# The sign of a float64 weight: a mask on VectorE, or a copy to float16 on ScalarE

## The chip, the cores and the metric

One core of one Trainium2 chip runs the whole program. The time is device microseconds of one execution, the median over several; the kernel before has three runs, 1212.31, 1214.31 and 1215.85 us. The profile is of one more execution.

## The reference

Three stages run one after the other, each on the output of the one before:

```python
# attention: q, k, v of 4 x 8 heads x 768 x 64, 4 sinks, window 128, float32
keep = is_sink | in_window
scores = np.where(keep, scale * (q @ k.T), -1e9)
a = softmax(scores);  x = a @ v            # -> 3072 tokens x 512

# MLP: w_in (512 x 2048) and w_out (2048 x 512) are float64
h = x @ w_in
g = h - np.tanh(h)
y = g @ w_out                              # -> float32

# MoE: 8 experts, 384 tokens each, assigned greedily by the sorted logits
logits = y @ w_gate
out[tok] = np.maximum(y[tok] @ w1[e], 0) @ w2[e]
```

`w_in` and `w_out` are a float32 array times a NumPy scalar, which makes them float64, and the kernel is given them so.

## The kernel before

TensorE multiplies in a reduced float32 format, so every float32 operand is split into a leading part and a remainder, and a product is three matmuls (leading by leading, remainder by leading, leading by remainder).

The tokens are worked on in eight units of 384. For each unit `u` a loop over 16 blocks `f` of the hidden size does `mlp_h` (lines 368 to 388: `h`, the tanh on ScalarE, `g`, `gh`, `gl`) and `mlp_y` (lines 390 to 414, line 402 is its matmul). Between these steps the attention of the next unit is spread: `scores` (line 269; matmuls 278 and 279, VectorE's line 287, ScalarE's exponential 288, VectorE's reciprocal 292, scaling 298), `transp` (319 to 322, tiles `ath` and `atl`), `sinks` (324; ScalarE makes the first half of `skT` in line 331, VectorE the second in 332) and `av` (335; matmul 351, then `xt` on ScalarE in 359, `xf` on VectorE in 360, `xh` in 363 on ScalarE, `xl` in 364 on VectorE). The matmul with `skT` is the last of each sum of `av`.

The float64 weights lie in DRAM as pairs of 32-bit words, and each piece is loaded as such a pair tile: 128 partitions x 1024 weights x 2 words. `leading` makes float32 of a piece. Word 1 holds the sign, the exponent and the upper bits of the mantissa. ScalarE scales it by 2^-112 as if it were a float32 (line 127), which leaves the exponent where an integer shift by three needs it. VectorE shifts word 0 right by 29, so that three bits are left (line 128), then puts the sign, which the later shift of word 1 would lose, into bit 31 of word 0 by a mask (line 129), and joins the two words by shift and or (line 131). The halves of a pair are counted 0 to 3 by the name `half`; half 3 is the upper half of word 1, half 1 the upper half of word 0, so bit 15 of half 1 is bit 31 of word 0.

`leading` is called 24 times: eight times in `split_win` for `w_in` (tile `winr`), eight in `split_wout` for `w_out` (tile `wor`), both before 180 us, and eight times in `gate_weights` (tile `wtr`), which works out `w_out` times `w_gate` between 300 and 560 us while the units 2 to 4 run. After each call ScalarE copies the leading part out (lines 146, 165, 454) and GpSimd subtracts for the remainder (147, 166, 455). The pair tiles of `w_out` and of the gates share one buffer, and the result of `leading` has two.

The order of the instructions on each engine is set by the framework's scheduler for the attention, the MLP and the gates; each engine then runs its list strictly in that order. The MoE part behind it is written out in an order of its own.

Of the kernel before, what the change touches and what calls it, by code (L numbers as in the profile page):

```python
# [10 lines left out]
F32 = mybir.dt.float32  # L11
F32R = mybir.dt.float32r
I32 = mybir.dt.int32
U16 = mybir.dt.uint16
BF = mybir.dt.bfloat16
F16 = mybir.dt.float16
AF = mybir.ActivationFunctionType
OP = mybir.AluOpType
# [15 lines left out]
def raw(t):  # L34
    return t.bitcast(F32)
# [3 lines left out]
def attn_mlp_moe(ctx, tc, qT, kP, v, w_in, w_out, w_outT, w_gate, w1, w2, out):  # L39
    nc = tc.nc  # L40
# [81 lines left out]
    def leading(pairs, n):  # L122


        hi, lo = pairs[:, :, :, 1], pairs[:, :, :, 0]
        half = pairs.rearrange("p a b t -> p a (b t)").bitcast(U16).rearrange("p a (b t) -> p a b t", t=4)
        nc.scalar.activation(raw(hi), raw(hi), AF.Copy, scale=2.0 ** -112)
        nc.vector.tensor_scalar(lo, lo, 29, None, op0=OP.logical_shift_right)
        nc.vector.tensor_scalar(half[:, :, :, 1], half[:, :, :, 3], 0x8000, None, op0=OP.bitwise_and)
        t = st.tile([P] + n, I32, name="f1")  # L130
        nc.vector.scalar_tensor_tensor(t, hi, 3, lo, op0=OP.logical_shift_left, op1=OP.bitwise_or)
        return t.bitcast(F32)
# [10 lines left out]
    def split_win(j):  # L143
        f1 = leading(WINR[j], [NC, 256])
        t = wts.tile([P, 2, NC, 256], F32R, name=f"win{j}", tag=f"win{j}")
        nc.scalar.copy(t[:, 0], f1)
        nc.gpsimd.tensor_sub(t[:, 1], f1, raw(t)[:, 0])
        WIN[j] = t
# [13 lines left out]
    def split_wout(j):  # L162
        f1 = leading(WOR[j], [2, C])
        t = wop.tile([P, 2, C], F32R, name=f"wo{j}")
        nc.scalar.copy(t, f1)
        nc.gpsimd.tensor_sub(f1, f1, raw(t))
        nc.sync.dma_start(wol_d[2 * j:2 * j + 2].rearrange("f p c -> p f c"), f1)
        WO[2 * j], WO[2 * j + 1] = t[:, 0], t[:, 1]
# [278 lines left out]
    def gate_weights(j):  # L447
        t = st.tile([P, NC, 256, 2], I32, name="wtr", tag="wor", bufs=1)
        nc.sync.dma_start(t.rearrange("p c f t -> p c (f t)"),
                          w_outT.bitcast(I32).rearrange("(c p) f -> p c f", p=P)[:, :, j * 512:(j + 1) * 512])  # L450
        yield
        f1 = leading(t, [NC, 256])
        t = st.tile([P, 2, NC, 256], F32R, name="wts_", tag="wor", bufs=1)
        nc.scalar.copy(t[:, 0], f1)
        nc.gpsimd.tensor_sub(t[:, 1], f1, raw(t)[:, 0])
        yield
        o = psA.tile([P, 512], F32, name="o")[:16, :256]
        for c in range(NC):
            for h in range(2):
                nc.tensor.matmul(o, wg[:, c], t[:, h, c], start=(c + h == 0), stop=(c == NC - 1 and h == 1))  # L460
        r = st.tile([16, 256], F32, name="wpr", tag="f1")
        nc.scalar.copy(r, o)
        yield
        t = psA.tile([P, 2, 16], F32, name="wpt", tag="t")
        for h in range(2):
            nc.tensor.transpose(t[:, h], r[:, h * P:(h + 1) * P], ident[:16, :16])
        s1 = st.tile([P, 2, 8], F32, name="wps", bufs=1)
        s2 = st.tile([P, 2, 8], F32, name="wpq", bufs=1)
        nc.scalar.copy(s1, t[:, :, 8:])
        nc.vector.tensor_add(s2, t[:, :, :8], s1)  # L470
        d = WPS[:, 2 * j:2 * j + 2]
        nc.vector.tensor_copy(d[:, :, :8], s2)
        nc.vector.tensor_sub(d[:, :, 8:], s2, raw(d)[:, :, :8])
        yield
# [43 lines left out]
    pairs = [(u, p) for u in range(NU) for p in range(4)]  # L518
# [650 lines left out]
```

## Time and profile before

| what | value |
|---|---|
| median of three runs | 1214.31 us |
| profiled execution: time, span | 1212.97 us, 1211.3 us |
| mean granted TensorE clock | 0.964 |
| busy share: TensorE, VectorE, ScalarE, GpSimd | 92%, 65%, 52%, 42% |
| line 129: runs, busy in total | 24, 38.88 us |

The span runs from the first to the last instruction; what the profiled execution took beyond it lies around it. The busy shares are over the whole span. The granted clock is the share of TensorE's full speed that the chip allowed, 1.00 in most of the run and less in the first 180 us.

### The profile page before, as it was taken

The numbers are of one execution on the slowest core, as the hardware profiler recorded it, in microseconds if no ns is written. First come the engines' busy times: TensorE is split into PE (matmuls) and PEld (weight loads), VectorE is DVE, ScalarE is ACT, GpSimd is POOL, SyncE is SP. The second block draws the span as 40 slices with busy tenths as digits, with TensorE's granted clock in tenths as the row PEclk, the third lists the DMA queues.
The fourth block names the chain that finished last, engine by engine and source line by source line (L and its number), as shares of the span: only waits on it lengthen the run. The fifth ranks groups of instructions, "written<-read, shape, count | busy, mean of one in ns | idle before, by whom it ended". The sixth has DMA issues, their size and how long they took to land.

```text
span 1211.3 us, 19574 instructions
## 1 busy us (share of the span) xinstructions
PE 1119.3 (92%) x6484; PEld 950.3 (78%) x6484; DVE 788.1 (65%) x2164; ACT 634.5 (52%) x1541; POOL 513.7 (42%) x616
## 2 busy tenths in 40 slices
PE   4677799999999999999999999998989999998997
PEld 3456588888888778888888888886677888887986
DVE  6779985656756667565665665455787878778321
ACT  6876666556655566665655665441224433343421
POOL 6367653324333344334332333100137765676830
PEclk9868989999999999999999999998979999998999
DMA  7554454233442434342332322111634564346500
GB/s 215 174 167 163 163 191 119 78 83 114 129 132 68 132 96 131 117 144 73 102 91 76 116 77 81 44 44 30 223 116 129 166 192 140 100 145 209 171 30 27
DMA packets 87606, 145.29 MB, mean 120 GB/s; under 512 B 9680, under 2 KB 32208, under 8 KB 87504
## 3 DMA queue, kind: packets, MB, share of 16 engines
q1 hardware_dynamic: 83664, 131.45, 35.5%
q0 software_dynamic: 3840, 12.59, 3.2%
q8 instruction: 51, 0.84, 0.3%
q14 instruction: 51, 0.42, 0.1%
HBM read 127.22 MB, written 16.78 MB: 119 GB/s over the span
## 4 chain that ended last, share of the span: by engine, by line
PE 71%; DVE 5%; issue 3%; DMA 3%; ACT 2%; POOL 1%; POOLq 0%; SPq 0%; ACTq 0%; DVEq 0%
PE y L402 18%; PE h L976 10%; PE o L1003 6%; PE h L375 6%; PE h L373 6%; PE h L374 6%; PE o L351 4%; PE o L1007 3%; PE t L319 2%; DMA wtr<-in_w_outT_dram 2%; PE s L278 2%; PE s L279 1%; DMA wl<-wol_d 1%; PE search L678 1%; PE o L429 1%
## 5 line engine op out<-in xcount | busy, mean ns | idle before, releaser
L891 POOL TENSOR_TENSOR w<-wraw,w 128x512 fp32r<-128x512 f32 x120 | 150.9, 1287 | 84.6 <-ACT w L885 83.6
L373 PE MATMUL h<-xh,win 128*128 128x384 f32 x512 | 178.7, 350 | 0.4 <-ACT xh L363 0.3
L375 PE MATMUL h<-xh,win 128*128 128x384 f32 x512 | 178.1, 348 | 0.0
L374 PE MATMUL h<-xl,win 128*128 128x384 f32 x512 | 175.4, 343 | 1.7 <-DVE xl L364 1.7
L976 PE MATMUL h<-mxh,w 128*128 128x384 f32 x512 | 147.1, 346 | 0.0
L402 PE MATMUL y<-wo,gl 128*128 128x512 f32 x336 | 141.5, 422 | 0.0
L402 PE MATMUL y<-wl,gh 128*128 128x512 f32 x336 | 136.3, 406 | 0.0
L402 PE MATMUL y<-wo,gh 128*128 128x512 f32 x336 | 134.9, 403 | 1.5 <-ACT gh L386 1.5
L300 POOL TENSOR_SCALAR a<-a,stat 128x260 f32<-128x260 f32 (+2 forms) x168 | 94.6, 576 | 79.7 <-DVE stat L292 74.0
L288 ACT ACTIVATE a<-sm,stat 128x260 f32<-128x260 f32 (+2 forms) x192 | 94.5, 492 | 40.9 <-DVE stat L287 38.3
L287 DVE CUSTOM_DVE_ANT_0 sm<-s,m 128x260 f32<-128x260 f32 (+2 forms) x192 | 76.9, 401 | 51.6 <-PE s L279 43.1
L1003 PE MATMUL o<-w,hh 128*128 128x512 f32 x384 | 108.7, 404 | 0.0
L982 ACT ACTIVATE hh<-h 128x384 fp32r<-128x384 f32 x64 | 31.5, 492 | 142.3 <-PE h L976 137.4
L373 PEld LDWEIGHTS h<-xh,win 128*128 128x128 f32 x512 | 97.7, 191 | 7.2 <-ACT xh L363 1.5
L374 PEld LDWEIGHTS h<-xl,win 128*128 128x128 f32 x512 | 97.8, 191 | 6.9 <-DVE xl L364 2.5
L380 DVE TENSOR_TENSOR g<-h,g 128x384 f32<-128x384 f32 x128 | 71.2, 556 | 46.9 <-ACT g L379 46.3
L250 POOL TENSOR_TENSOR kl<-k,kh 128x388 fp32r<-128x388 f32 (+1 forms) x64 | 81.3, 1277 | 45.8 <-ACT kh L249 45.8
L375 PEld LDWEIGHTS h<-xh,win 128*128 128x128 f32 x512 | 97.9, 191 | 2.5 <-issue 1.5
L379 ACT ACTIVATE g<-h 128x384 f32<-128x384 f32 x128 | 62.1, 485 | 68.9 <-PE h L375 64.0
L976 PEld LDWEIGHTS h<-mxh,w 128*128 128x128 f32 x512 | 94.1, 191 | 2.4
L264 POOL TENSOR_TENSOR vs<-vr,vs 128x192 fp32r<-128x192 f32 (+1 forms) x64 | 46.5, 733 | 114.2 <-ACT vs L263 113.3
L885 ACT CAST w<-wraw 128x512 fp32r<-128x512 f32 x128 | 73.5, 619 | 38.4 <-DMA wraw<-in_w_dram 38.1
(261 smaller groups left out, 2646.1 us busy)
## 6 DMA issues: line engine op xcount, KB each, us to landing
wl<-wol_d SPq DMA_DIRECT2D x128, 256.0 KB, 2.8
wraw<-in_w_dram SPq DMA_DIRECT2D x128, 256.0 KB, 3.6
k<-in_k_dram SPq DMA_DIRECT2D x64, 131.0 KB, 2.9
winr<-in_w_in_dram SPq DMA_DIRECT2D x8, 1024.0 KB
wor<-in_w_out_dram SPq DMA_DIRECT2D x8, 1024.0 KB, 4.9
wtr<-in_w_outT_dram SPq DMA_DIRECT2D x8, 1024.0 KB, 5.7
k<-in_k_dram SPq DMA_DIRECT2D x64, 97.0 KB, 2.5
q<-in_q_dram SPq DMA_DIRECT2D x32, 192.0 KB, 2.7
```

The lines of the kernel that those rows point to most:

```text
L250: nc.gpsimd.tensor_sub(kl[:, :kn], k2[:, :kn], raw(kh)[:, :kn])
L287: nc.vector.tensor_tensor_reduce(sm[:, :n], s[:, :n], m, 1.0, 3e38, OP.add, OP.min, r[:, 0, hh:hh + 1])
L288: nc.scalar.activation(a[:, hh, :n], sm[:, :n], AF.Exp, bias=r[:, 0, hh:hh + 1], scale=-1.0, accum_out=r[:, 1, hh:hh + 1])
L300: nc.gpsimd.tensor_scalar(a[:, j, :n], a[:, j, :n], r[:, 3, j:j + 1], 1.0, op0=OP.mult, op1=OP.mult)
L373: nc.tensor.matmul(hp, w, xh[:, c], start=(c == 0), stop=False)
L374: nc.tensor.matmul(hp, w, xl[:, c], start=False, stop=False)
L375: nc.tensor.matmul(hp, win(f, 1, c), xh[:, c], start=False, stop=(c == NC - 1))
L402: mm = nc.tensor.matmul(y, m[:, ts], w, start=(f == 0 and w is hi and m is gh), stop=(f == NF - 1 and m is gl))
L885: nc.scalar.copy(W[n, q][:, 0, a], WR[n, q, a])
L891: (dve if mine else nc.gpsimd).tensor_sub(t[:, 1], r, raw(t)[:, 0])
L976: nc.tensor.matmul(hp, w[:, h, c, fs], x[:, c], start=(c + k == 0), stop=(c == NC - 1 and k == 2))
L1003: nc.tensor.matmul(o, hh[:, t * P:(t + 1) * P], w, start=(f + k == 0), stop=False)
```

## The change

The mask on VectorE goes. In its place ScalarE copies the scaled word 1, read as float32, into half 1 read as float16. The scaled word's magnitude is about 2^-112, far under the least float16, so that the copy yields a zero with the word's sign: bit 15 set or not.

```diff
--- before.py
+++ after.py
@@ -11,7 +11,6 @@
 F32 = mybir.dt.float32
 F32R = mybir.dt.float32r
 I32 = mybir.dt.int32
-U16 = mybir.dt.uint16
 BF = mybir.dt.bfloat16
 F16 = mybir.dt.float16
 AF = mybir.ActivationFunctionType
@@ -123,10 +122,11 @@
 
 
         hi, lo = pairs[:, :, :, 1], pairs[:, :, :, 0]
-        half = pairs.rearrange("p a b t -> p a (b t)").bitcast(U16).rearrange("p a (b t) -> p a b t", t=4)
+        half = pairs.rearrange("p a b t -> p a (b t)").bitcast(F16).rearrange("p a (b t) -> p a b t", t=4)
         nc.scalar.activation(raw(hi), raw(hi), AF.Copy, scale=2.0 ** -112)
         nc.vector.tensor_scalar(lo, lo, 29, None, op0=OP.logical_shift_right)
-        nc.vector.tensor_scalar(half[:, :, :, 1], half[:, :, :, 3], 0x8000, None, op0=OP.bitwise_and)
+
+        nc.scalar.copy(half[:, :, :, 1], raw(hi))
         t = st.tile([P] + n, I32, name="f1")
         nc.vector.scalar_tensor_tensor(t, hi, 3, lo, op0=OP.logical_shift_left, op1=OP.bitwise_or)
         return t.bitcast(F32)
```

The copy of line 129 reads what line 127's scaling wrote (both on ScalarE), and writes into the word that VectorE's shift has written, so it waits for the shift; VectorE's line 131 then waits for the copy. In the new kernel the scaling is line 126, the shift line 127; the other lines keep their numbers.

VectorE in the second gate, the shift of `wtr` to line 360's first addition, as a piece of the difference from before to after:

```order
 L322 TENSOR_TENSOR atl<-t,ath 128x2x256
-L128 TENSOR_SCALAR wtr<-wtr 128x1024
-L380 TENSOR_TENSOR g<-h,g 128x384
-L129 TENSOR_SCALAR wtr<-wtr 128x1024
+L127 TENSOR_SCALAR wtr<-wtr 128x1024
+L380 TENSOR_TENSOR g<-h,g 128x384
 L332 TENSOR_TENSOR skT<-s,skT 8x384
 L387 TENSOR_TENSOR gl<-g,gh 128x384
 L131 SCALAR_TENSOR_TENSOR f_3882<-wtr 128x1024
-L360 TENSOR_TENSOR xf<-o,xt 64x384 x2
```

The mask that stood ahead of `skT` (line 332) has gone, and the join of line 131 stays behind `gl` (line 387).

ScalarE in the same place, from the tanh of line 379 to `xt` of line 359:

```order
 L379 ACTIVATE g<-h 128x384
-L127 ACTIVATE wtr<-wtr 128x1024
-L331 CAST skT<-s 8x384
-L386 CAST gh<-g 128x384
+L126 ACTIVATE wtr<-wtr 128x1024
+L331 CAST skT<-s 8x384
+L386 CAST gh<-g 128x384
+L129 CAST wtr<-wtr 128x1024
 L359 COPY xt<-o 64x384
```

The new copy (CAST) stands behind `skT` and `gh`, and ahead of `xt`.

ScalarE in the early part, among the splits of `w_in` and `w_out` (`winr_392` is a pair tile, `f_806` a joined float32 piece):

```order
-L359 COPY xt<-o 64x384
-L127 ACTIVATE winr_392<-winr_392 128x1024
-L359 COPY xt<-o 64x384
-L288 ACTIVATE a,stat<-sm,stat 128x260
-L321 CAST ath<-t 128x2x256
+L359 COPY xt<-o 64x384 x2
+L129 CAST wor<-wor 128x1024
+L363 CAST xh<-xf 128x384
+L129 CAST winr_392<-winr_392 128x1024
 L165 CAST wo_808<-f_806 128x1024
-L363 CAST xh<-xf 128x384
```

Before, a scaling of `winr` and the weight copy of line 165 stood between the first `xt` (359) and `xh` (363); now it is the new copy for `wor` that stands between them.

## Rows read from the trace of the kernel before

**Rows 1.** The page's first part: busy us, share of the span, instructions.

```profile
PE 1119.3 (92%) x6484; PEld 950.3 (78%) x6484; DVE 788.1 (65%) x2164; ACT 634.5 (52%) x1541; POOL 513.7 (42%) x616
```

**Rows 2.** Windows: length, busy us (count) by engine, granted clock, DMA share, GB/s.

```profile
30.00:60.00 30.00, 18.49 (x79) 14.71 (x78) 23.41 (x64) 24.08 (x77) 9.60 (x11) 0.83 0.53 169
60.00:90.00 30.00, 21.63 (x81) 16.45 (x81) 23.17 (x41) 22.07 (x52) 18.30 (x15) 0.66 0.55 175
90.00:150.00 60.00, 46.16 (x219) 37.13 (x217) 57.12 (x69) 37.44 (x73) 43.60 (x32) 0.91 0.49 165
150.00:180.00 30.00, 27.13 (x135) 23.76 (x136) 24.56 (x46) 20.11 (x47) 16.67 (x16) 0.89 0.53 180
180.00:300.00 120.00, 119.80 (x666) 103.81 (x666) 72.98 (x190) 74.46 (x204) 40.66 (x68) 1.00 0.35 100
300.00:560.00 260.00, 249.88 (x1404) 213.73 (x1403) 169.64 (x413) 162.07 (x414) 99.49 (x137) 0.99 0.38 115
```

**Rows 3.** Windows of line 129's instructions alone: length, VectorE busy us (count).

```profile
0.00:60.00 60.00, 5.97 (x3) 0.91 0.62 192
60.00:90.00 30.00, 4.46 (x3) 0.66 0.55 175
90.00:150.00 60.00, 15.22 (x8) 0.91 0.49 165
...
300.00:560.00 260.00, 10.58 (x8) 0.99 0.38 115
```

**Rows 4.** Line 129 by tile: ns least, median, most; first and last start us.

```profile
L129 DVE TENSOR_SCALAR winr<-winr x8: 1309/1454/3332, 12.0 to 116.1; 128x1024 uint16<-128x1024 uint16 x8
...
L129 DVE TENSOR_SCALAR wtr<-wtr x8: 1305/1324/1336, 314.0 to 544.6; 128x1024 uint16<-128x1024 uint16 x8
```

**Rows 5.** Timeline, 96 us: start, us, engine, line, operation.

```profile
96.12 2.41 POOL L166 TENSOR_TENSOR f<-f,wo 128x1024 f32<-128x1024 f32 x1
...
96.38 3.33 DVE L129 TENSOR_SCALAR winr<-winr 128x1024 uint16<-128x1024 uint16 x1
```

**Rows 6.** Line 127, tile wor: ns least, median, most.

```profile
L127 ACT ACTIVATE wor<-wor x8: 1140/1156/1171, 71.3 to 170.9; 128x1024 f32<-128x1024 f32 x8
```

**Rows 7.** Line 146: ns least, median, most.

```profile
L146 ACT CAST win<-f x8: 1030/1042/1048, 26.1 to 141.3; 128x1024 fp32r<-128x1024 f32 x8
```

**Rows 8.** TensorE's waits, 60 to 180 us: us in total, times, longest.

```profile
PE s L278 <- DVE stat L287: 7.9, 5, 3.6
...
PE o L351 <- DVE atl L322: 3.0, 1, 3.0
```

**Rows 9.** Timeline, 30 to 34 us; in brackets the idle time before and its releaser.

```profile
30.38 3.10 DVE L129 TENSOR_SCALAR winr<-winr 128x1024 uint16<-128x1024 uint16 x1
...
33.99 0.77 PE L319 MATMUL t<-ident,a 128*128 128x128 f32 x2 [3.08 <-ACT a L298]
```

**Rows 10.** TensorE's waits, 300 to 560 us.

```profile
PE o L351 <- DVE skT L332: 7.4, 7, 1.8
PE o L351 <- DVE xf L360: 1.5, 3, 0.8
```

**Rows 11.** Timeline of gate 2 (its load landed at 337.08).

```profile
338.14 0.45 ACT L331 CAST skT<-s 8x384 fp32r<-8x384 f32 x1
...
338.31 1.31 DVE L129 TENSOR_SCALAR wtr<-wtr 128x1024 uint16<-128x1024 uint16 x1
...
339.65 0.55 DVE L332 TENSOR_TENSOR skT<-s,skT 8x384 fp32r<-8x384 f32 x1
...
340.25 0.44 PE L351 MATMUL o<-skT,vsk 40*128 40x384 f32 x1 [1.45 <-DVE skT L332]
```

**Rows 12.** Windows behind three of the gates, columns as in rows 2.

```profile
337.00:347.00 10.00, 8.55 (x43) 7.55 (x41) 5.98 (x9) 4.98 (x9) 3.46 (x3) 0.83 0.10 29
364.00:375.00 11.00, 9.22 (x46) 8.17 (x44) 6.35 (x11) 5.58 (x11) 3.83 (x3) 0.84 0.10 29
443.00:453.00 10.00, 8.95 (x52) 7.51 (x50) 6.87 (x14) 6.44 (x14) 3.05 (x3) 1.00 0.18 58
```


## The prediction

> **What bounds the kernel now.** I read the page's first part, then the windows stage by stage, then the waits. TensorE is busy for 92% of the span and VectorE for 65% [rows 1], but these are means over stages with different limits. The windows separate them [rows 2]: from 180 to 300 us TensorE works 119.80 of 120 us, so nothing that VectorE saves there reaches the end. Before that it isn't full: 18.49 of 30 us from 30 on, 21.63 of 30 from 60 on, 46.16 of 60 from 90 on, 27.13 of 30 from 150 on. In the stretch from 90 to 150 us the engine nearest to full is VectorE, with 57.12 of 60 us, while ScalarE has 37.44 and GpSimd 43.60. From 30 to 60 us ScalarE (24.08) and VectorE (23.41) are level. That early part is one place where the edit can pay; the splits of `w_in` and `w_out` lie in it. The other is 300 to 560 us, where TensorE has 249.88 of 260 us and the eight `gate_weights` run.
>
> **What is removed.** The mask of line 129 runs 24 times. Its own busy time by window [rows 3] is 5.97 us before 60 us (3 of them), 4.46 (3) from 60 to 90, 15.22 (8) from 90 to 150, and 10.58 (8) among the gates; two more lie between 150 and 180. Undisturbed, one takes about 1.31 us [rows 4]: the eight of the gates lie between 1305 and 1336 ns, and early ones reach 3332. The long ones coincide with GpSimd [rows 5]: line 166's subtraction runs from 96.12 for 2.41 us, to 98.53; the mask that starts at 96.38 takes 3.33 us, which is 2.15 to that end and 1.18 more, about a whole mask.
>
> **What is added.** ScalarE gets 24 copies of 128x1024 with float32 in and half words out, strided by 8 bytes on both sides. The trace has no such copy. Its nearest rows are the scaling of line 127 with the same strided source (1156 ns, between 1140 and 1171, [rows 6]) and the contiguous copy of line 146 (1042 ns, [rows 7]). I take 1.1 us; two-byte writes could make it dearer, and for that the trace has only VectorE's mask itself, the one operation on half words in it, at 1.31 us undisturbed, so the bounds are 1.04 and 1.31. The copy waits for VectorE's shift, and line 131 on VectorE waits for the copy; behind that wait stand the attention's rows on VectorE.
>
> The Trainium skill, "ScalarE: Activation LUTs", section "Rules for kernel authors", speaks against the edit: cheap element-wise work belongs on VectorE, which it puts at up to about 3 times ScalarE's speed in bf16. The rows here don't bear that factor out for a strided half-word mask (1.31 us against ScalarE's 1.04 to 1.16 on 1024 columns). Were the factor true here, a copy would take about 3.9 us by an estimate from that page and a mask's 1.31, and the 16 early ones would put 63 us on ScalarE.
>
> **Term A, the early part (0 to 180 us).** From 90 to 150 us VectorE falls from 57.12 to about 41.9 us (15.22 less), ScalarE rises from 37.44 by 8 x 1.1 = 8.8 to 46.2, and TensorE stays at 46.16 [rows 2, 3]. Three engines are then between 42 and 46. If the fullest engine sets the length, the 60 us become no less than about 47: a gain of at most 13. If a mixed stage stays at the fill that 30 to 60 us shows, where the fullest engine has 24.08 of 30 us, which is 80%, the length is 46.2 / 0.80 = 57.6 and the gain 2.4. I take the middle, 7 us: the stage is led by one engine now and by none later, but the attention's chain passes through all four. Waits agree in kind: from 60 to 180 us TensorE waits 7.9 us for line 287's results and 3.0 for `atl`, both VectorE's [rows 8], 10.9 us together.
>
> The Trainium skill, "SBUF — State Buffer", section "SBUF: two separate sides", calls the port pair that VectorE shares with GpSimd an exclusive lock for a whole instruction, whose loser blocks fully. The 3.33 us mask beside a GpSimd subtraction agrees. By that rule the excess over 1.31 us would pass to the next VectorE instruction, and the 90 to 150 stretch would lose 8 x 1.31 = 10.5 us of VectorE work instead of 15.2; it would then be 46.6 of VectorE against 46.2 of ScalarE, and the bound of 13 would hardly move.
>
> From 60 to 90 us neither engine is full (23.17 and 22.07 of 30 us, TensorE at a granted clock of 0.66); three masks go and three copies come, and I take -1. For 150 to 180 us, with two masks, -0.5. For 0 to 60 us a mask of 3.10 us at 30.38 holds up the reciprocal of line 292, for which ScalarE's line 298 and then TensorE wait; TensorE's transpose at 33.99 had waited 3.08 us [rows 9]. That goes, but two more copies, 2.2 us, come onto the fullest engine of 30 to 60 us; I take -0.5, between +2.2 and -4. The new order of ScalarE there puts a copy of `wor` between the attention's `xt` and `xh`, so that the MLP's first matmul waits for a copy that itself waits for VectorE's shift; but `xh` had a scaling and another weight copy ahead of it before. Term A is -7 - 1 - 0.5 - 0.5 = -9 us, between 0 (2.4 of gain, 2.2 given back) and about -21 (13, 4, and the 4.46 us of the three masks).
>
> **Term B, the gates (300 to 560 us).** TensorE waits 7.4 us in 7 times for `skT` of line 332 [rows 10], and gate 2 shows why [rows 11]: the mask starts at 338.31 and takes 1.31 us, line 332 stands behind it on VectorE and starts at 339.65, and TensorE's product with `skT` starts at 340.25 after 1.45 us of waiting. ScalarE's half of `skT` (line 331) started at 338.14 and took 0.45, so line 332 could start at 338.59, 1.06 us earlier; in the new order it stands ahead, with nothing but line 380 between it and the shift. Two of the seven waits can give the full 1.06 (1.45 here and the longest, 1.8); the other five sum to 7.4 - 1.45 - 1.8 = 4.15 and can give no more than that. That bounds the gain by 6.3. Another releaser stands close behind: TensorE also waits 1.5 us in three times for `xf` of line 360, and ScalarE's next `xt` now comes behind the copy, 1.1 us later at most. I take -5.
>
> After gate 2's wait the granted clock of the ten microseconds from 337 is 0.83, after gate 3's 0.84, while after a later one (443 to 453) it stays at 1.00 [rows 12]. Each fall costs about 10 x 0.17 = 1.7 us. Whether the shorter idle leaves the clock up can't be read before; I take half of 3.4, -1.5. Term B is -6.5, between 0 and -9.7.
>
> **Sum.** -9 - 6.5 = -15.5 us on the profiled execution's 1212.97 gives 1197.5. The median of the runs shown lies 1.3 us above that execution, so I predict **1199 us**. A change of 0.3% is 3.6 us: below 1210.7 is faster, above 1217.9 slower.
>
> **Rivals.**
> - *Only the gates pay.* ScalarE takes VectorE's place in the early part, as in 30 to 60 us, and term A comes to nothing: 1214.3 - 6.5 = 1207.8. For it: that stretch's level engines. Against it: 57.12 against 37.44 from 90 to 150 us.
> - *Nothing reaches the end.* TensorE, 92% busy, takes back in its full stretch whatever is gained, or line 131's wait for the copy replaces the mask: about 1214. Against it: a stretch that TensorE fills can't give back time saved ahead of it, since its work stays the same.
> - *More than the sum.* The early clock, 0.66 from 60 to 90 and 0.91 from 90 to 150 us [rows 2], rises as TensorE waits less. 30 us at 0.91 instead of 0.66 would shorten TensorE's 21.63 us by 21.63 x (1 - 0.66/0.91) = 5.9, and A goes to its upper half, -13: 1214.3 - 13 - 5.9 - 6.5 = 1188.9, and about 1190 as the first two overlap.
> - *Slower.* ScalarE becomes the engine that everything waits for: 16 early copies x 1.16 = 18.6 us in front of the attention's exponentials and `xh`, against 10.9 us of waits for VectorE that go: +7.7, and with B at nothing 1222. It decides from the point at which ScalarE, with its copies, is fuller than VectorE was: 57.12 from 90 to 150 us needs copies of (57.12 - 37.44) / 8 = 2.46 us, twice the upper bound. So it is unlikely.
> - *The edit doesn't save what it says.* The half words could be written so slowly that a copy reaches 2.46 us; then ScalarE is where VectorE was, and the time stays at about 1214 less the gates. By the factor in the Trainium skill, weighed above, the copy would be past that. It is part of the cases of no change and of slower.
>
> **How the numbers follow.** Forecast (1193 to 1206): 0.55. Only the gates: 0.17. Nothing: 0.08. More than the sum: 0.13. Slower: 0.07. The range from 1188 to 1211 leaves out the last case, most of the nothing and the tail of the fourth. Faster takes the first, second and fourth, less a little that lands within 0.3%: 0.84. Same is 0.09, slower 0.07.
>
> **What would show it.** In the changed profile: copies of line 129 on ScalarE near 1.1 us; VectorE near 42 us of work per stretch of its eight masks, the stretch from 90 us on shorter by some 7 us; waits for `skT` near 2 us in place of 7.4; a granted clock above 0.66 in the worst early stretch. Wrong would be copies over 2 us, waits of VectorE's line 131 for line 129 that sum to more than what the masks took, or an early stretch as long as before with ScalarE full.

## The result and the profile after

The changed kernel takes 1227.8 us (median of 11 runs, 1222.47 to 1232.95), the kernel before 1214.18 us (11 runs, 1209.27 to 1219.2). The ratio is 1.0118 with a 95% interval from 1.0096 to 1.0139: about 14 us slower, where 15 us faster was forecast.

The first part of the page of the changed kernel, with the busy time, share and instruction count of each engine:

```profile
span 1224.8 us, 19544 instructions
...
PE 1120.9 (92%) x6484; PEld 948.3 (77%) x6484; DVE 746.4 (61%) x2140; ACT 688.5 (56%) x1565; POOL 503.1 (41%) x616
```

VectorE has lost 41.7 us of work against [rows 1], and ScalarE has 54.0 us more than the 634.5 of before. 24 copies of 1.1 us would be 26. The view of line 129 shows why (least, median and most in ns; the last line is who waited):

```profile
L129 ACT CAST winr<-winr x8: 2487/2560/2649, 14.5 to 145.8; 128x1024 f16<-128x1024 f32 x8
L129 ACT CAST wor<-wor x8: 2494/2563/2720, 79.2 to 181.9; 128x1024 f16<-128x1024 f32 x8
...
L129 ACT CAST wtr<-wtr x8: 2477/2504/2594, 324.4 to 558.1; 128x1024 f16<-128x1024 f32 x8
...
who waited for it (us, times):
  DVE f L131: 21.4, 12
```

A copy takes 2.5 us and not 1.1. The windows of the changed kernel, columns as in [rows 2]:

```profile
60.00:90.00 30.00, 18.55 (x69) 14.37 (x68) 17.66 (x40) 27.00 (x55) 13.22 (x11) 0.61 0.50 165
90.00:150.00 60.00, 44.42 (x211) 35.17 (x211) 39.05 (x62) 53.97 (x80) 36.32 (x34) 0.93 0.52 171
...
300.00:560.00 260.00, 245.47 (x1390) 208.54 (x1390) 156.57 (x403) 179.39 (x420) 95.87 (x135) 1.00 0.39 118
```

From 90 to 150 us VectorE and ScalarE have changed places: VectorE falls from 57.12 to 39.05 us and ScalarE rises from 37.44 to 53.97. From 60 to 90 us ScalarE works 27.00 of 30 us and TensorE only 18.55 (21.63 before).

TensorE's waits from 60 to 180 us in the changed kernel:

```profile
PE t L319 <- POOL a L300: 6.9, 3, 4.7
PE o L351 <- POOL vs L264: 6.1, 4, 2.4
PE y L402 <- DVE gl L387: 4.6, 4, 2.1
...
PE s L278 <- DVE stat L287: 3.5, 4, 1.4
```

Two rows of the same view before the change, beside those of [rows 8]:

```profile
PE t L319 <- POOL a L300: 4.8, 5, 1.6
...
PE o L351 <- POOL vs L264: 1.5, 2, 1.0
```

All rows of the view sum to 31.7 us after the change and to 25.0 before it. The waits for VectorE's line 287 fall from 7.9 to 3.5 us, and those for GpSimd's lines 300 and 264 and for line 387 grow by more.

Where the time goes is read from one mark that every kernel passes at the same places of its program, the starts of ScalarE's 32 copies to `xh` (line 363, four per unit), by the timelines of one profiled execution each. The table has the start before and how much later or earlier the changed kernel and five of the experiments come there (us):

| copy to `xh` | before | changed | e_early | e_gates | e_word | e_worde | e_wordg |
|---|---|---|---|---|---|---|---|
| 1st | 34.63 | -1.24 | -3.23 | +0.39 | -4.18 | -4.37 | +1.31 |
| 8th | 199.85 | +10.31 | +7.35 | -0.43 | -0.22 | -4.68 | +2.33 |
| 12th | 291.54 | +10.23 | +7.39 | -0.43 | -0.24 | -4.69 | +2.35 |
| 20th | 497.80 | +10.28 | +7.03 | +0.59 | -6.32 | -4.36 | -5.43 |
| 32nd | 784.90 | +13.60 | +8.17 | +6.54 | -7.35 | -4.81 | -5.83 |

10.3 us of the loss arise before 200 us, none while TensorE is full (8th to 12th), and 3.3 us behind the 20th copy. Kernels with the same early program stand apart at the 8th copy: e_gates and e_wordg, whose early splits are those of before, by 2.8 us (-0.4 and +2.3), e_word and e_worde by 4.5 us (-0.2 and -4.7). So one profile's early part is sure to some 4 to 5 us only. Behind the 32nd copy all seven kernels take 425.8 to 427.4 us, also those that leave the signs of weights out.

The timeline of gate 2 after the change (the load lands at 349.35) shows the new wait:

```profile
350.42 0.45 ACT L331 CAST skT<-s 8x384 fp32r<-8x384 f32 x1
...
350.90 0.55 DVE L332 TENSOR_TENSOR skT<-s,skT 8x384 fp32r<-8x384 f32 x1 [0.38 <-ACT skT L331]
351.19 2.51 ACT L129 CAST wtr<-wtr 128x1024 f16<-128x1024 f32 x1
351.48 0.56 DVE L387 TENSOR_TENSOR gl<-g,gh 128x384 fp32r<-128x384 f32 x1
...
351.50 0.44 PE L351 MATMUL o<-skT,vsk 40*128 40x384 f32 x1 [1.33 <-DVE skT L332]
353.72 0.48 ACT L359 COPY xt<-o 64x384 f32<-64x384 f32 x1
353.73 1.23 DVE L131 SCALAR_TENSOR_TENSOR f<-wtr 128x1024 int32<-128x1024 int32 x1 [1.69 <-ACT wtr L129]
354.87 0.54 DVE L360 TENSOR_TENSOR xf<-o,xt 64x384 f32<-64x384 f32 x1
```

From the landing to the product with `skT` it is 351.50 - 349.35 = 2.15 us, against 340.25 - 337.08 = 3.17 before [rows 11]: 1.02 earlier, as worked out. But behind it `xt` stands behind the copy on ScalarE (353.72), the join waits 1.69 us for the copy on VectorE, and `xf` comes behind both. TensorE's waits from 300 to 580 us in the changed kernel:

```profile
PE o L351 <- DVE xf L360: 8.9, 8, 1.5
PE o L351 <- DVE skT L332: 5.7, 7, 1.8
```

The waits for `xf` grow from 1.5 to 8.9 us [rows 10]. All waits of the stretch sum to 14.6 us, against 9.8 before, where one more row stands beside the two of [rows 10]:

```profile
PE s L278 <- DVE stat L287: 0.9, 1, 0.9
```

That is 4.8 us more. On the other side, the two falls of the granted clock of [rows 12] are gone (1.00 from 340 to 380 us in the changed kernel), and one stands behind the last gate:

```profile
560.00:570.00 10.00, 9.72 (x50) 8.52 (x49) 5.88 (x15) 7.61 (x18) 4.84 (x6) 0.83 0.22 67
```

With the prediction's estimate of 1.7 us a fall, 4.8 - 3.4 + 1.7 = 3.1 us, about the 13.60 - 10.23 = 3.4 us that the table has from the 12th to the 32nd copy. It is also why the table stands still from the 12th to the 20th copy, although six of the eight gates lie there: what the waits lose there, the two falls give back.

### The profile page after: what moved, and what is told of

Same layout as the page of the kernel before. It is cut to its first block, busy times and chain, and to the rows that moved or that the text cites. A ratio compares the mean times of both kernels' runs of the same rounds, so it can differ in the third digit from the quotient of the medians.

```text
span 1224.8 us, 19544 instructions
## 1 busy us (share of the span) xinstructions
PE 1120.9 (92%) x6484; PEld 948.3 (77%) x6484; DVE 746.4 (61%) x2140; ACT 688.5 (56%) x1565; POOL 503.1 (41%) x616
## 4 chain that ended last, share of the span: by engine, by line
PE 73%; ACT 8%; issue 5%; DMA 5%; DVE 4%; POOL 3%; SPq 0%; POOLq 0%; ACTq 0%; DVEq 0%
PE y L402 18%; PE h L976 10%; PE o L1003 6%; PE h L375 6%; PE h L374 6%; PE h L373 6%; PE o L351 5%; PE o L1007 3%; DMA wtr<-in_w_outT_dram 3%; PE t L319 3%; PE s L278 2%; PE s L279 2%; ACT wtr L129 2%; DMA wl<-wol_d 1%; DVE f L131 1%
## 5 line engine op out<-in xcount | busy, mean ns | idle before, releaser
L300 POOL TENSOR_SCALAR a<-a,stat 128x260 f32<-128x260 f32 (+2 forms) x168 | 89.6, 546 | 78.9 <-DVE stat L292 73.1
L264 POOL TENSOR_TENSOR vs<-vr,vs 128x192 fp32r<-128x192 f32 (+1 forms) x64 | 43.8, 691 | 110.0 <-ACT vs L263 109.9
```

The source lines that it names most:

```text
L300: nc.gpsimd.tensor_scalar(a[:, j, :n], a[:, j, :n], r[:, 3, j:j + 1], 1.0, op0=OP.mult, op1=OP.mult)
```

## The experiments

Every kernel below keeps the rest of the program. The times are medians, with the ratio to the kernel before on the same chip and its 95% interval.

**The copy by itself.** A program with nothing but one load of pairs and line 129's copy in several forms, three times each (`dh`, `db`: a tile of pairs seen as float16 and bfloat16 halves; `wide`: contiguous; `flat` read as float16 at every second half):

```python
nc.scalar.copy(dh[:, :, 1], hi)              # line 62: as in the change
nc.scalar.copy(dh[:, :, 1], one[:, :, 1])    # line 63: values of 0.5
nc.scalar.copy(dst[:, :, 0], hi)             # line 65: whole words, 8 bytes apart
nc.scalar.copy(wide, hi)                     # line 66: contiguous float16
nc.scalar.copy(db[:, :, 1], hi)              # line 67: bfloat16
nc.scalar.copy(dh[:, :512, 1], hi[:, :512])  # line 68: half as many
nc.scalar.copy(fh[:, :, 1], hi)              # line 75: halves 4 bytes apart
```

> This kernel computes nothing of the reference: it loads one piece of pairs and runs the copy of line 129 alone, three times each in several forms of 128x1024, so its time says nothing and only durations are read. Theory A (the write is what costs: two bytes into every eighth byte): the same float32 source into 4-byte words 8 bytes apart takes about 1.15 us, float16 into a contiguous tile about 1.05, bfloat16 into every eighth byte 2.5 like float16, and 512 columns about half, 1.3 us. Theory B (the conversion costs, since the values lie far under float16's least): copies of 0.5 into the same half words take about 1.15 us and the scaled weights 2.5. Theory C (any 16-bit output on ScalarE costs): the contiguous float16 copy takes 2.5 as well.

Durations of each line in that program, then two of VectorE's (line 71 is the old mask, line 72 a copy of whole words):

```profile
L62 ACT CAST dst<-big x3: 2455/2455/2457, 7.1 to 34.5; 128x1024 f16<-128x1024 f32 x3
...
L63 ACT CAST dst<-one x3: 2455/2455/2516, 10.4 to 37.0; 128x1024 f16<-128x1024 f32 x3
...
L65 ACT COPY dst<-big x3: 1088/1088/1155, 16.8 to 42.0; 128x1024 f32<-128x1024 f32 x3
...
L66 ACT CAST wide<-big x3: 1132/1188/1197, 9.3 to 15.8; 128x1024 f16<-128x1024 f32 x3
...
L67 ACT CAST dst<-big x3: 2516/2532/2563, 18.0 to 44.2; 128x1024 bf16<-128x1024 f32 x3
...
L68 ACT CAST dst<-big x3: 1351/1353/1392, 20.6 to 47.6; 128x512 f16<-128x512 f32 x3
...
L75 ACT CAST flat<-big x3: 1322/1463/1478, 43.0 to 48.7; 128x1024 f16<-128x1024 f32 x3
...
L71 DVE TENSOR_SCALAR dst<-big x3: 1299/1300/1300, 50.4 to 57.2; 128x1024 uint16<-128x1024 uint16 x3
...
L72 DVE COPY dst<-big x3: 696/696/696, 51.7 to 58.5; 128x1024 f32<-128x1024 f32 x3
```

The values don't matter (line 63), the conversion doesn't (line 66), the stride of the source or of whole words doesn't (line 65). Two bytes written into every eighth cost 2455 ns, with nothing else running. At every fourth byte it is 1.3 to 1.5 us. From 512 to 1024 columns the cost grows by 2455 - 1353 = 1102 ns, 2.15 ns a column. Theory A holds; B and C fall. VectorE pays for such half words too: 1300 ns against 696 for whole words. There, too, it is the write: VectorE's cast of the same float32 source takes 1301 ns into those half words and 694 into a contiguous tile.

**The same kernel with a 4-byte write (e_word).** Every engine's order is that of the changed kernel; only the write is wide. A zero replaces word 0: the low three bits go, and the sign too, since this zero carries none.

```diff
-        nc.scalar.copy(half[:, :, :, 1], raw(hi))
+        nc.scalar.activation(raw(lo), raw(hi), AF.Copy, scale=0.0)
```

> The changed kernel with line 129 writing a signed zero over the whole 4-byte word 0 (scale 0.0, float32 out), which drops the low three mantissa bits of the weights; the order of every engine stays that of the changed kernel. Theory 1 (only the copy's size was wrong: 2.5 us where 1.1 was taken): the copy takes about 1.15 us, ScalarE's work from 90 to 150 us falls from 54.0 to about 43 us, and the kernel lands near the forecast, 1197 to 1207 us. Theory 2 (a step on ScalarE between the scaling and the join costs whatever its length, because VectorE waits for it at line 131 with the attention's rows behind it): 1214 us or more.

1202.93 us (0.9911, 0.9887 to 0.9935): 11 us faster than before, 25 us faster than the changed kernel, with the same instructions waiting for one another. ScalarE's line 129 takes 1.13 to 1.14 us at the median. Theory 1 holds, theory 2 falls. The profiled execution, 1205.47 us, is the slowest of its six, so the table's -7.35 is less than the 11 us of the medians. The windows of this kernel:

```profile
60.00:90.00 30.00, 18.93 (x75) 15.11 (x75) 20.58 (x40) 26.79 (x57) 18.00 (x18) 0.67 0.51 157
90.00:150.00 60.00, 52.24 (x234) 42.39 (x233) 38.73 (x63) 44.28 (x82) 34.61 (x28) 0.84 0.48 164
```

From 60 to 90 us ScalarE is as full with the cheap copy (26.79 of 30 us) as with the dear one (27.00), and TensorE works no more (18.93 and 18.55).

**One part at a time.** First the change as it is, in one part of the program, with the mask in the other (`by_copy` is given by each caller of `leading`):

```diff
-        nc.vector.tensor_scalar(half[:, :, :, 1], ...)
+        nc.scalar.copy(half16[:, :, :, 1], raw(hi)) if by_copy else nc.vector.tensor_scalar(half[:, :, :, 1], ...)
```

Gates only:

> The copy in the eight gates only, the mask in the 16 early splits. By the profile after, 3.4 us of the loss arise behind 300 us: theory 1 (each part costs by its own copies) expects 1214 + 3.4 = 1217 to 1218 us. Theory 3 (the loss behind 300 us comes from the altered phase of the early part and not from the gates): 1212 to 1215, or a gain of some 5 us as forecast for the gates.

1219.83 us (1.0041, 1.0020 to 1.0062): +5.7. The profile of this kernel loses 7.0 us from the 12th to the 32nd copy. TensorE's waits from 300 to 580 us are 3.9 us more than before (13.7). The granted clock falls behind gate 2 as before, not behind gate 3, and is 0.50, the lower of its two levels, for ten microseconds behind the last gate:

```profile
550.00:560.00 10.00, 9.57 (x33) 8.03 (x32) 4.26 (x10) 5.56 (x14) 3.74 (x3) 0.50 0.16 52
```

By the same estimate that fall costs 5 us, and 3.9 + 5 - 1.7 = 7.2. So what the gates lose depends on where the clock falls as well, and that differs from kernel to kernel. Early splits only:

> The copy in the 16 early splits only, the mask in the gates. Theory 1: 1214 + 10.2 = 1224 us, the early part ten microseconds longer with ScalarE the full engine from 60 to 150 us. Theory 3: near 1228 us, all of the loss. If the loss came from the gates alone, 1214.

1222.12 us (1.0080, 1.0052 to 1.0108): +8.0. Together 13.7, which is the change's loss by medians (13.6); that they agree to a tenth is luck, since the intervals are 2.5 and 3.4 us to either side. Theory 3 falls.

The early part again, by its two weights. `w_out` only, and then `w_in` only:

> The copy in the eight splits of w_out only, the mask elsewhere. Theory 1: ScalarE gets 8 x 2.5 = 20 us over the whole early part and VectorE loses 8 x 1.5 = 12; no window is fuller than before, 1210 to 1216 us. Theory 4: half of the early loss of 8.0, 1218.

1215.39 us (1.0016, 0.9999 to 1.0033): no difference that the runs can tell.

> The copy in the eight splits of w_in only. The first of them stand ahead of the first matmuls of the MLP, so a piece that comes 1.2 us later is felt at once. Theory 1: 1212 to 1218 us; theory 4: half of the early loss, 1218. If the two halves together give less than the loss of both (8.0), the loss starts where ScalarE is full, and not with each copy.

1221.87 us (1.0064, 1.0041 to 1.0087): +8.7, as much as both. So it isn't each copy that costs; theory 4 expected 1218 of either, and theory 1's 1212 to 1218 misses too. The loss hangs on the `w_in` pieces. That they cost because the MLP waits for them first was only argued, and this kernel's profile doesn't bear it out: it is 2.0 us ahead of before at the 1st copy to `xh`, 4.1 behind at the 4th and 8.9 at the 8th, and up to 200 us no wait of TensorE is for a piece of `w_in`. Two of its waits there, which were 11.7 and 0.3 us before, and one of its windows:

```profile
PE s L278 <- DVE stat L287: 14.9, 7, 4.0
...
PE h L373 <- ACT xh L363: 3.9, 1, 3.9
```

```profile
90.00:150.00 60.00, 46.13 (x205) 38.45 (x206) 46.60 (x69) 43.92 (x77) 38.66 (x33) 0.81 0.52 171
```

Neither VectorE nor ScalarE is above 47 of 60 us here, and the loss is as large as with all 16 copies. The expectation's other reading, that the loss starts where ScalarE is full, doesn't hold either. The clock is lower than before in this stretch (0.81 against 0.91 in [rows 2]); how much of the loss that is wasn't separated.

Half the columns of each early piece by copy, half by mask:

```diff
+        m = half.shape[1] // 2
+        nc.scalar.copy(half16[:, m:, :, 1], hi[:, m:])
+        nc.vector.tensor_scalar(half[:, :m, :, 1], half[:, :m, :, 3], 0x8000, None, op0=OP.bitwise_and)
```

> In the 16 early splits ScalarE copies the sign for 512 of the 1024 weights of a partition and VectorE masks the other 512; the gates keep the mask. By the lone copies a piece costs ScalarE 1.35 us and VectorE 0.7. Theory 1 (the fuller of the two engines sets the early part): from 90 to 150 us VectorE 57.1 - 8 x 0.65 = 52, ScalarE 37.4 + 8 x 1.35 = 48, both under what either had before: 1209 to 1214 us. Theory 4 (all time added to ScalarE there costs, since TensorE's waits are for chains that pass through it): half of the early copy's loss, 1218.

1216.67 us (1.0020, 1.0002 to 1.0038). This kernel's window:

```profile
90.00:150.00 60.00, 46.85 (x231) 38.30 (x230) 46.96 (x75) 48.78 (x85) 39.35 (x32) 0.94 0.54 178
```

The profiled execution, 1221.38 us, is the slowest of the twelve. Neither engine is above 49 of 60 us, and nothing is gained: theory 1 in its simple form, that the fuller of two engines sets the early part, misses here, and theory 4's 1218 is nearer.

**The 4-byte write in one part at a time.** The forecast's two terms with the price that it assumed. Gates only:

> The 4-byte form (a zero over word 0, which leaves the sign and the low three bits out) in the eight gates only, the mask in the early splits. By the profile of the kernel with the 4-byte form everywhere, its gain of 7.3 us arises almost wholly behind 300 us. Theory 1: 1214 - 7 = 1207 us, near the forecast's 6.5 us for the gates. Theory 5 (the gain behind 300 us was luck of the early part's phase): 1212 or more.

1206.56 us (0.9953, 0.9934 to 0.9973): -5.8 against 1212.32, the median of before in this group of runs. Theory 5 falls. TensorE's waits from 300 to 580 us are one row:

```profile
PE o L351 <- DVE skT L332: 5.3, 7, 1.7
```

The waits for `xf` (1.5) and for line 287 (0.9) are gone, those for `skT` are 2.1 us less, and the granted clock behind gates 2 and 3 stays up, against 0.83 and 0.84 in [rows 12]:

```profile
337.00:347.00 10.00, 8.29 (x48) 7.05 (x47) 4.64 (x7) 6.18 (x10) 1.81 (x3) 1.00 0.32 104
364.00:375.00 11.00, 10.46 (x61) 8.85 (x60) 6.68 (x14) 8.53 (x18) 3.79 (x3) 1.00 0.14 45
```

With 1.7 us for each of the two falls that is 1.5 + 0.9 + 2.1 + 3.4 = 7.9 us; from the 12th to the 32nd copy of the table this kernel gains 2.35 + 5.83 = 8.2. What is left of the wait in gate 2 is the load: ScalarE and VectorE both wait for it, and `skT` stands behind them on both.

```profile
340.40 1.17 ACT L127 ACTIVATE wtr<-wtr 128x1024 f32<-128x1024 f32 x1 [1.40 <-DMA wtr<-in_w_outT_dram]
340.42 0.70 DVE L128 TENSOR_SCALAR wtr<-wtr 128x1024 int32<-128x1024 int32 x1 [2.01 <-DMA wtr<-in_w_outT_dram]
...
342.54 0.44 PE L351 MATMUL o<-skT,vsk 40*128 40x384 f32 x1 [1.71 <-DVE skT L332]
```

Early splits only:

> The 4-byte form in the 16 early splits only, the mask in the gates. The forecast's term A (VectorE leads the early part, 9 us to gain at a copy of 1.1 us) expects 1205 us. If the early part isn't led by VectorE's fill but by chains through ScalarE and GpSimd, 1210 to 1214.

1208.69 us (0.9977, 0.9954 to 1.0001): -3.6, not sure to be other than zero, and not the 9 of term A. TensorE's waits from 60 to 180 us in this kernel:

```profile
PE t L319 <- POOL a L300: 6.6, 3, 4.8
PE o L351 <- POOL vs L264: 4.9, 4, 2.5
PE y L402 <- DVE gl L387: 3.7, 4, 2.1
...
PE s L278 <- DVE stat L287: 1.0, 2, 0.8
```

The waits for VectorE's line 287 fall from 7.9 to 1.0 us and the one for `atl` is gone [rows 8]. GpSimd takes their place: the waits for its lines 300 and 264 were 4.8 and 1.5 us before and are 6.6 and 4.9 now. In all the waits fall from 25.0 to 21.6 us. The table has this kernel 4.4 us ahead at the 1st copy already and 4.7 at the 8th: nearly all that its profile gains early is gained in the first 35 us, where the mask of 3.10 us at 30.38 [rows 9] has gone.

**Other ways to the same end.** Sign and shift in one instruction of VectorE, with ScalarE writing the zero into the contiguous result tile. Its zero carries no sign either, so as run this kernel leaves the signs out and isn't the full computation that the expectation calls it.

```diff
+        t = st.tile([P] + n, I32, name="f1")
+        nc.scalar.activation(raw(t), raw(hi), AF.Copy, scale=2.0 ** -100)
+        nc.vector.scalar_tensor_tensor(t, lo, 29, t, op0=OP.logical_shift_right, op1=OP.bitwise_or)
+        nc.vector.scalar_tensor_tensor(t, hi, 3, t, op0=OP.logical_shift_left, op1=OP.bitwise_or)
```

> A full computation in another form: ScalarE writes the signed zero as float32 into the contiguous tile that line 131 fills anyway, and VectorE takes shift and sign in one instruction (word 0 shifted, or the zero) and the join in the next. ScalarE gets 1.05 to 1.15 us, VectorE has 2 x 1.22 = 2.44 us a piece in place of 0.70 + 1.31 + 1.22 = 3.23. If four-byte writes keep ScalarE below full (theory 1), VectorE's 24 x 0.79 = 19 us less should give about half of the gain of the 4-byte copy, 1206 to 1211 us. If a join that now waits for two steps on ScalarE costs (theory 2), 1214 or more.

1219.32 us (1.0052, 1.0029 to 1.0074). This misses theory 1's 1206 to 1211, with a ScalarE step as cheap as in e_word. Theory 2's 1214 or more fits the time, but the order of all engines differs from both kernels from the first microseconds on, and which of that costs wasn't separated; it stays open.

The kernel before with its masks, and the gates' splits later in the loop:

```diff
-                    push(u * NS + gs + k * 8, lambda g=gws[j]: next(g))
+                    push(u * NS + gs + k * 8 + 8 * (k > 0), lambda g=gws[j]: next(g))
```

> The kernel before, with the mask everywhere; only the three later steps of each gate come eight places later in the loop. VectorE's list then has line 332 (skT) ahead of the gate's shift and mask in all gates after the first, so that neither the load's landing nor the mask stands ahead of skT. Theory 1 (the gates' waits are a matter of what stands ahead of skT and xf): most of the 9.8 us of TensorE's waits from 300 to 560 us go, 1205 to 1209 us. Rival: the mask now stands ahead of xf of line 360, and the wait moves there, 1212 to 1215.

1212.41 us against 1212.32 (1.0001, 0.9985 to 1.0018). The rival holds; the wait moves to `xf`, as this kernel's rows from 300 to 580 us show:

```profile
PE o L351 <- DVE xf L360: 7.2, 8, 1.4
...
PE o L351 <- DVE skT L332: 0.7, 2, 0.3
```

Fourteen places in place of eight:

> As the one with eight places, with fourteen: the gate's shift and mask come behind the first xf of the head pair as well, and the load has had six places more to land. Theory 1: 1204 to 1208 us; rival: the second xf behind the mask waits, 1212 to 1215.

1219.3 us (1.0059, 1.0039 to 1.0078), slower than either theory said. In the same stretch TensorE now waits 7.4 us in nine times for line 287, against 0.9 before. The mask now stands ahead of the attention's next scores; that this is why TensorE waits was read from the order and not tested.

## Why the prediction was wrong

**The step that failed is the price of the copy**, under "What is added": "I take 1.1 us; two-byte writes could make it dearer, [...] so the bounds are 1.04 and 1.31". It is 2.50 to 2.56 us at the median in the kernel and 2.455 alone. The bounds took the strided source from one row and the width from none: no ScalarE row of the trace wrote half words, and VectorE's mask was taken as the upper end though it is another engine's. (It isn't "the one operation on half words" there either: VectorE's lines 666 and 765 write bfloat16.) That mask did carry a hint in the trace of before that was passed over: 1.31 us for half words [rows 4], where the shift of whole words next to it takes 0.70:

```profile
337.09 0.70 DVE L128 TENSOR_SCALAR wtr<-wtr 128x1024 int32<-128x1024 int32 x1 [0.70 <-DMA wtr<-in_w_outT_dram]
```

That the price made the result is shown by e_word: with the order unchanged and a copy of 1.13 us the kernel comes to 1202.93 us, inside the forecast's 1193 to 1206. Half words cost VectorE 1.9 times, and ScalarE 2455 / 1088 = 2.26 times.

The rule of the Trainium skill that was set aside ("ScalarE: Activation LUTs", "Rules for kernel authors") had the direction: for this form ScalarE takes 2455 / 1300 = 1.9 times VectorE's time. The contiguous row of 1042 ns that spoke against it [rows 7] is of another form.

**The rival "Slower" had the direction; its figure is luck.** It came to 1222 with early copies of 1.16 us, 18.6 us against 10.9 us of waits that go. With copies of that price the early splits lose nothing (1208.69), and with the measured 2.56 us its own sum would be 16 x 2.56 - 10.9 = 30 us, where the early splits lose 8.0. The copies did reach the 2.46 us at which ScalarE would be as full as VectorE was (53.97 against 57.12 us), and the rival called that unlikely. But that fill isn't what decides: with the copies of `w_in` alone ScalarE has 43.92 of 60 us, and as much is lost. Which chain carries the early loss stays open.

**Removal of the mask**: right. From 90 to 150 us VectorE's work was to be 42 us and is 39.05; in the kernel with cheap copies 38.73. Over the whole run VectorE loses 41.7 us against the masks' 38.88, so the excess of the long masks didn't pass to other instructions, and the 46.6 us that the prediction worked out for that case aren't borne out.

**Term A (-9)**: wrong by more than the price. With a copy of 1.1 us the early part gives 3.6 us (not sure to be other than zero), within the term's bounds (0 to 21) but well under the 7 taken for 90 to 150 us alone. By the two profiles, each sure to some 4 us, nothing is gained there: with the cheap copy the 1st copy to `xh` comes 4.2 and 4.4 us earlier (e_word, e_worde), where the term took 0.5 for all of the first 60 us, and from there to the 8th e_worde gains 0.3 and e_word loses 4.0. The early clock, which "More than the sum" hoped would rise, stays at 0.61 to 0.67 from 60 to 90 us in the changed kernel, e_word and e_worde. "Led by one engine now and by none later" was the wrong half: GpSimd's waits were listed in the view of waits and not counted. Such a stretch has a next engine, and its waits grow by 5.2 us (lines 300 and 264) as VectorE's shrink.

**Term B (-6.5)**: right in size at the price assumed, 5.8 measured, and in the parts that it named, 1.02 us earlier from landing to product and two falls of the clock less. The expected 2 us of waits for `skT` was wrong (5.3): the load comes later against TensorE's progress when the rest is quicker (ScalarE waits for it 2.9 us in three gates, 0.5 in one before), and the chain from it to `skT` was read from its landing on. At 2.5 us the same place loses, through `xt` behind the copy on ScalarE and `xf` behind the join on VectorE, which the prediction named and priced at 1.1 us at most.

**"Nothing reaches the end"** (TensorE takes it back) is refuted both ways: the table's differences hold from the 8th to the 12th copy.

Of the kernels run, the 4-byte form everywhere is the fastest, but it leaves the signs out; none that keeps them beat the kernel before.

## What to carry to other kernels

Price an operation by a row of the same engine, the same width of element and the same stride of its output; where one of the three is missing, the bound is open, and a small program with nothing but that operation settles it. When work moves off the fullest engine, list who is waited for next in the stretch before counting the gain: here GpSimd stood behind VectorE and gave back more than half. And follow a wait behind a load from the load's landing both ways, to what stands behind it on each engine.

## What the runs showed of the hardware

- ScalarE writing 1024 two-byte elements 8 bytes apart takes 2.455 us alone, 1.3 to 1.5 at 4 bytes apart, 1.13 to 1.20 contiguous, while four-byte elements 8 bytes apart take 1.09. The Trainium skill, "ScalarE: Activation LUTs", section "What ACT_TABLE_LOAD costs", gives 186 ns and 0.833 ns a column for an instruction of this kind, fp32 and bf16 alike; by an estimate from it 1024 columns take 1.04 us, which agrees with [rows 7] and not with half words 8 bytes apart, whose slope here is 2.15 ns a column.
- VectorE shows the same for half words, more mildly: 1.30 us against 0.70 for whole words at the same stride.
